# Two attention blocks on one core: reciprocals as exp(-ln) on ScalarE, the first rows of x in two halves, and new thresholds for the order of work

## The chip, the core and the metric

The kernel runs on one core of a Trainium2 chip. Its engines run side by side, each through its own list of instructions in order: TensorE (PE in the profile; PEld is its weight load), VectorE (DVE), ScalarE (ACT), GpSimd (POOL) and SyncE (SP), which here only issues DMAs. They wait for one another by semaphores. The metric is the device time of one execution in microseconds (us).

## The reference

Two independent blocks read their own x of 2048 rows by 512 columns; their results stand side by side in the output. Both have 32 heads of width 16.

```python
# A: softmax attention
scores = einsum("bhqd,bhkd->bhqk", q, k) * Dh ** -0.5
o = einsum("bhqk,bhkd->bhqd", softmax(scores), v);  a = o @ wo
# B: linear attention with learned features
phi_q = concat([softmax(q @ w_phi), softmax(-(q @ w_phi))]);  phi_k likewise
kv = einsum("bhsf,bhsd->bhfd", phi_k, v);  z = phi_k.sum over s
o = (phi_q @ kv) / (phi_q @ z + 1e-6);  b = o @ wo
```

Block A is nearly all of the work: 32 x 2048 x 2048 scores, each computed, put through an exponential, and summed.

## The kernel before, in words

**Block A.** Heads are taken four at a time (8 groups g). A *unit* is one group with a stretch of 128 or 256 queries; there are 73. Each unit goes through two passes over its scores, because the exponential needs the row maximum first.

- *Pass D*: PE computes scores with queries on the partitions (line 971), 512 keys to a PSUM bank, and DVE reduces one bank or two at a time to row maxima (line 1084, tile `part`). For some query blocks ("z") ACT first takes half of the work (`zS`, line 1011) and DVE joins it (line 1078).
- The maxima of a unit are joined on GpSimd, transposed by DMA and written as extra rows into the masked queries `QZ`, so that the next pass gets score minus maximum out of the matmul itself.
- *Pass E*: PE computes the scores again with keys on the partitions (line 1234), and ACT writes the exponential of one or two banks into a ring of 34 tiles `pT` (line 1246).
- *PV*: PE multiplies `pT` with the values, which carry a column of ones, so that the row sum comes out as a 17th row (line 1324).
- `finish_unit` then evacuates the result to `X`, moves the row sums by DMA into a compact tile `lr` (line 1381), takes their reciprocal on DVE (line 1384: 128 x 8 elements for a unit of 256 queries, 128 x 4 for one of 128), spreads them by five DMAs over `Yd`, and GpSimd multiplies `X` by `Yd` into `QT` (line 1403), where the output projection (line 1419) reads them. `X`, `lr` and `Yd` have two buffers each, one for even units and one for odd. The last three units go by `finish_last`, with a reciprocal of 128 x 128 straight from PSUM (line 1356).

**Block B** runs in the shadow of block A from about 240 us on, mostly on GpSimd. In `q_norm`, GpSimd adds 1e-6 to the 32 denominators of each row (`den_t`, line 1793), DVE takes the reciprocal (line 1795, 128 x 32), and GpSimd multiplies (line 1798). This happens 16 times.

**The start.** SP loads x in five pieces (two of 256 rows, three of 512) and the rest of the weights; ACT's queue loads the first columns of the weights for K and Q. PE runs six idle matmuls, turns the first 512 rows (line 374), DVE and ACT copy the four results (lines 381 and 383), and then the projections of K and Q for these rows (line 710), the masked queries of the first three units (`first_qz`, line 734), and the first scores follow. `pad_copy` (line 361) spreads the weights of Q and K into padded tiles.

**What sets the order.** From 7.6 us on the order on every engine is written by an *account* (`_Account`, made when the kernel is built). It keeps a clock for each engine, with a cost in us for each kind of work, and appends an instruction to an engine's list when the account's clock says that it is free. `task` gives ACT, DVE, GpSimd and SP work with a priority (lower goes first); an evacuation may go to ACT or to DVE (`choose`). `pick_pe` and `fill_cand` decide what PE does next: scores of pass D or E, PV, a projection job, or a filling matmul. They read a table of thresholds, `TH0`, overlaid with one row of `TH` for every 60 us. Those that the text speaks of are: `SINGLE` and `ESINGLE` (how little queued work DVE or ACT must have before PE fills one bank instead of two), `DCAP` and `ECAP` (how much queued work is the most), `COL` and `INCOL` (how much work both must have before PE turns to PV and projections), `PV_START`, `PV_LOW` and `PVN` (how full the ring of `pT` must be), and `BAL` (when DVE takes an evacuation). Semaphore waits are derived from the same dependencies, so the order is fixed, and the times at run time are those of the chip.

Of the kernel before, what the change touches and what calls it, by code (L numbers as in the profile page):

```python
# [213 lines left out]
def bass_concat_heads__softmax_full_mha__linear_kernel_hedgehog__prompt_kernel(  # L214
# [21 lines left out]
    with contextlib.ExitStack() as es:  # L236
# [81 lines left out]
        t_wa = {}  # L318
# [9 lines left out]
        def load_x(name, b0, b1):  # L328
            t_xs[name] = P.dma("sp", dsem("xs%d" % name), lambda e: e.dma_start(
                xs[:, b0:b1, :], A_x[0][128 * b0:128 * b1, :].rearrange("(b p) n -> p b n", p=128)))  # L330
# [5 lines left out]
        load_x(2, 4, 8)  # L336
# [27 lines left out]
        t_wqp = pad_copy(WQp, 0, t_wq0)  # L364
# [5 lines left out]

        pe_idle(6, [t_zmv, t_ones])
        for rb in range(4):
            for ct in range(4):
                t_turn = P.op("pe", lambda e, rb=rb, ct=ct: e.matmul(
                    PS[:, ct, 128 * rb:128 * rb + 128], xs[:, rb, ct * 128:ct * 128 + 128], ident[:, :],
                    start=True, stop=True), [t_xs[rb // 2], t_ident] if ct == 0 else [])
        pe_idle(2)
        t_x0 = []
        for ct in range(4):
            if ct % 2 == 0:  # L380
                t_x0.append(P.op("dve", lambda e, ct=ct: e.tensor_copy(xAT[:, ct, 0:512], PS[:, ct, :]), [t_turn]))
            else:
                t_x0.append(P.op("act", lambda e, ct=ct: e.activation(
                    xAT[:, ct, 0:512], PS[:, ct, :], ACT.Copy), [t_turn]))
# [17 lines left out]
        for r in range(4):  # L402
# [8 lines left out]
            {'SINGLE': 1.013, 'ESINGLE': 1.026, 'ZBIAS': 0.274, 'DBIAS': 0.27, 'ZREST': 0.238},  # L411
            {'SINGLE': 0.647, 'UA': 0.441, 'RF': 0.465, 'REPM': 0.115, 'PV_LOW': 6, 'DCAP': 2.442, 'ZBIAS': 0.207, 'BAL': 68.611},
            {'SINGLE': 1.013, 'UA': 0.408, 'REPM': 0.215, 'LHI': 0.119, 'DCAP': 1.302, 'ECAP': 1.815, 'ZBIAS': 0.315, 'DBIAS': 0.27, 'BAL': -28.613},
            {'SINGLE': 1.157, 'UA': 0.408, 'RF': 0.436, 'REPM': 0.215, 'LHI': 0.03, 'PV_START': 5, 'PV_LOW': 5, 'DCAP': 1.302, 'ECAP': 1.815, 'ZBIAS': 0.315, 'BAL': -28.613},
            {'SINGLE': 0.287, 'UA': 0.425, 'RF': 0.532, 'REPM': 0.196, 'LHARD': 0.35, 'LHI': 0.119, 'DCAP': 1.302, 'ECAP': 1.815, 'ZBIAS': 0.315, 'DBIAS': 0.27, 'BAL': -27.419},
            {'SINGLE': 1.157, 'UA': 0.408, 'RF': 0.436, 'REPM': 0.214, 'LHARD': 0.383, 'LHI': 0.03, 'PV_START': 5, 'PV_LOW': 5, 'PVN': 3, 'DCAP': 1.322, 'ECAP': 1.904, 'ZBIAS': 0.315, 'BAL': -27.335},
            {'COL': 0.708, 'SINGLE': 1.157, 'UA': 0.441, 'REPM': 0.196, 'LHI': 0.065, 'PVN': 3, 'DCAP': 2.495, 'ECAP': 1.461, 'ZBIAS': 0.315, 'DBIAS': 0.27, 'BAL': -27.419},
            {'ESINGLE': 1.165, 'RF': 0.62, 'REPM': 0.196, 'LHI': 0.065, 'ECAP': 1.185, 'ZBIAS': 0.049, 'DBIAS': 0.27, 'BAL': -27.419, 'ZREST': -0.23},
            {'ESINGLE': 1.2, 'RF': 0.62, 'REPM': 0.196, 'LHI': 0.122, 'ECAP': 1.185, 'ZBIAS': 0.049, 'DBIAS': 0.27, 'BAL': -27.419, 'ZREST': -0.23},
            {'COL': 0.63, 'INCOL': 0.753, 'ESINGLE': 1.097, 'RF': 0.436, 'REPM': 0.196, 'LHI': 0.079, 'JOBHOLD': 20.274, 'DCAP': 2.036, 'ECAP': 1.185, 'ZBIAS': 0.034, 'DBIAS': 0.314, 'BAL': -27.419, 'ZREST': -0.23},  # L420
            {'COL': 0.487, 'INCOL': 0.753, 'SINGLE': 0.633, 'ESINGLE': 1.097, 'RF': 0.596, 'REPM': 0.196, 'LHI': 0.079, 'JOBHOLD': 20.274, 'DCAP': 2.036, 'ECAP': 1.185, 'ZBIAS': 0.034, 'DBIAS': 0.334, 'BAL': -27.419, 'ZREST': -0.23},
            {'COL': 0.63, 'INCOL': 0.753, 'SINGLE': 0.663, 'ESINGLE': 1.097, 'UA': 0.458, 'RF': 0.676, 'REPM': 0.196, 'LHARD': 0.355, 'LHI': 0.246, 'JOBHOLD': 14.826, 'PV_START': 5, 'DCAP': 2.036, 'ECAP': 1.276, 'ZBIAS': 0.072, 'DBIAS': 0.278, 'BAL': -30.019, 'ZREST': -0.23},
            {'COL': 0.53, 'INCOL': 0.753, 'SINGLE': 0.674, 'ESINGLE': 1.097, 'UA': 0.442, 'RF': 0.67, 'REPM': 0.369, 'LHARD': 0.317, 'LHI': 0.259, 'JOBHOLD': 12.459, 'PV_START': 5, 'DCAP': 2.021, 'ECAP': 1.276, 'ZBIAS': 0.129, 'DBIAS': 0.278, 'BAL': -37.649, 'ZREST': -0.23},
            {'COL': 0.35, 'INCOL': 0.753, 'SINGLE': 0.749, 'ESINGLE': 1.097, 'UA': 0.433, 'RF': 0.67, 'REPM': 0.369, 'LHI': 0.259, 'JOBHOLD': 25, 'PV_START': 5, 'ECAP': 1.276, 'ZBIAS': 0.391, 'DBIAS': 0.278, 'BAL': -37.649, 'ZREST': -0.23},
            {'COL': 0.53, 'INCOL': 0.753, 'SINGLE': 0.749, 'ESINGLE': 1.097, 'UA': 0.442, 'RF': 0.67, 'REPM': 0.369, 'LHI': 0.259, 'JOBHOLD': 17.436, 'PV_START': 5, 'ECAP': 1.276, 'ZBIAS': 0.129, 'DBIAS': 0.278, 'BAL': -37.649, 'ZREST': -0.23},
            {'COL': 0.486, 'INCOL': 0.753, 'SINGLE': 0.638, 'ESINGLE': 1.097, 'UA': 0.442, 'RF': 0.67, 'REPM': 0.348, 'LHI': 0.259, 'JOBHOLD': 17.436, 'PV_START': 5, 'ECAP': 1.276, 'ZBIAS': 0.129, 'DBIAS': 0.278, 'BAL': -30.554, 'ZREST': -0.23},
            {'COL': 0.486, 'INCOL': 0.753, 'SINGLE': 0.638, 'ESINGLE': 1.097, 'UA': 0.442, 'RF': 0.67, 'REPM': 0.189, 'LHI': 0.259, 'JOBHOLD': 17.436, 'PV_START': 5, 'ECAP': 1.276, 'ZBIAS': 0.129, 'DBIAS': 0.278, 'BAL': -30.554, 'ZREST': -0.23},
            {'COL': 0.486, 'INCOL': 0.753, 'SINGLE': 0.735, 'ESINGLE': 1.057, 'UA': 0.442, 'RF': 0.648, 'REPM': 0.21, 'LHI': 0.234, 'JOBHOLD': 17.436, 'DCAP': 2.479, 'ECAP': 1.276, 'ZBIAS': 0.129, 'DBIAS': 0.278, 'BAL': -37.429, 'ZREST': -0.23},
            {'COL': 0.657, 'INCOL': 0.753, 'SINGLE': 0.735, 'ESINGLE': 1.057, 'UA': 0.442, 'RF': 0.648, 'REPM': 0.21, 'LHI': 0.234, 'JOBHOLD': 13.418, 'DCAP': 2.479, 'ECAP': 1.171, 'ZBIAS': 0.129, 'DBIAS': 0.278, 'BAL': -30.554, 'ZREST': -0.23},
            {'COL': 0.486, 'INCOL': 0.753, 'SINGLE': 0.933, 'ESINGLE': 1.057, 'UA': 0.442, 'RF': 0.61, 'REPM': 0.21, 'LHARD': 0.251, 'LHI': 0.285, 'JOBHOLD': 17.436, 'DCAP': 2.479, 'ECAP': 1.356, 'ZBIAS': 0.119, 'DBIAS': 0.111, 'BAL': -37.429, 'ZREST': -0.23},  # L430
# [4 lines left out]
        K.now = 7.6  # L435
# [3 lines left out]
        for e in K.free:  # L439
            K.free[e] = 7.6  # L440
# [32 lines left out]
        bank_tok = {ct: t_x0[ct] for ct in range(4)}  # L473
# [147 lines left out]
        area = []  # L621
# [68 lines left out]
        def proj(kind, a, c, at, prio):  # L690
            if kind == "v":
# [11 lines left out]
            else:  # L703
# [4 lines left out]

                def mm(e, b, ct):
                    return e.matmul(PS[:, b, :], wpad[:, ct, g, :], xAT[:, ct, c * 512:(c + 1) * 512],  # L710
                                    start=(ct == 0), stop=(ct == 3))
# [11 lines left out]
            job(at, [(2, 512, mm), (2, 512, lambda e, b, i: mm(e, b, i + 2))], fin, deps, prio)  # L723
# [3 lines left out]
        def first_qz(b, t):  # L727

            col = 0
            for u in range(3):  # L730
                w = units[u][2]

                def run(eng, u=u, w=w, col=col):
# [3 lines left out]
                    if u == 2:  # L737
# [4 lines left out]
                col += w  # L742
            QTt[(0, 0)] = qz_t[2]
# [73 lines left out]

        early = [("k", 0, 0), ("q", 0, 0)]
# [5 lines left out]
        at = 7.6  # L824
# [546 lines left out]
        def finish_unit(u, pt, bank):  # L1371
            if u >= NU - LASTU:
# [11 lines left out]
            pw_t[u] = K.task("dve", (0.115, 0.22), lambda eng: P.op("dve", lambda e: e.reciprocal(  # L1384
                lr[:, ub, 0:n], lr[:, ub, 0:n]), toks(d2)), d2, prio=-3.0, name="rec")
# [404 lines left out]
        def q_norm(st, cx):  # L1790
# [4 lines left out]
            t2 = K.task("dve", (0.265, 0.38), lambda eng: P.op("dve", lambda e: e.reciprocal(  # L1795
# [285 lines left out]
```

## Time and profile before

| | |
|---|---|
| time, median of 3 runs | 1199.13 us (1198.91 to 1201.43) |
| profiled execution: its time, its span | 1199.05 us, 1197.3 us |
| busy PE, DVE, ACT, POOL | 1117.4, 1170.3, 1149.8, 821.8 us |
| granted clock of TensorE | 0.999 |
| DVE: row maxima, line 1084 | 1118 instructions, 1130.0 us |
| ACT: exponentials, line 1246 | 1573 instructions, 1027.7 us |
| ACT: evacuations, line 560, from 60 to 1140 us | 214 instructions, 113.2 us |
| DVE: evacuations, line 563, in the whole span | 2 instructions, 1.1 us |

How to read it: the profile is one execution, with a record (start and duration) for each instruction. Busy time is the union of an engine's records. Records of neighbouring instructions overlap by some tenths of a microsecond, so the distance from one start to the next is what an instruction takes from a full engine. In a group of instructions the columns are line, engine, operation, tiles, shapes and count, then busy us and mean ns of one, then the engine's idle time just before them and what ended it. In a row of a stage the number in brackets behind a busy time is the count of instructions.

### The profile page before, as it was taken

What the parts mean: (1) busy time and instruction counts of PE and PEld (TensorE: products, weight loads), DVE (VectorE), ACT (ScalarE), POOL (GpSimd) and SP (SyncE); (2) the same over time, 40 slices, a digit from 0 to 9 for tenths busy, and PEclk for the clock granted to TensorE, in tenths of its full rate; (3) what the DMA queues carried; (4) which work ended last, traced back from release to release, by engine and by line L of the source; (5) the groups of instructions that cost most, each with busy time, mean ns of one, the idle gap of its engine ahead of it and who ended that gap; (6) DMA issues with size and microseconds to landing.
All of it is one profiled execution on the core that took longest, in us unless ns stands there. A gap on an engine that the chain in (4) does not pass through costs nothing.

```text
span 1197.3 us, 32106 instructions
## 1 busy us (share of the span) xinstructions
PE 1117.4 (93%) x13025; PEld 468.9 (39%) x13025; DVE 1170.3 (98%) x1290; ACT 1149.8 (96%) x1891; POOL 821.8 (69%) x1636
## 2 busy tenths in 40 slices
PE   8998999998999999999999998999999998899998
PEld 3433333343334333333433333333333333345555
DVE  8999999999999999999999999999999999999995
ACT  5898999999999999999999999999999999999997
POOL 8511211227888888888787887888888888888860
PEclk9999999999999999999999999999999999999999
DMA  5011221210002001001000101121112111111120
GB/s 142 9 25 43 42 48 32 43 38 8 8 14 35 8 6 26 13 10 22 12 7 17 25 7 22 22 49 31 29 34 33 35 34 27 20 29 37 33 30 18
DMA packets 104119, 33.61 MB, mean 28 GB/s; under 512 B 86692, under 2 KB 103972, under 8 KB 103972
## 3 DMA queue, kind: packets, MB, share of 16 engines
q1 hardware_dynamic: 102916, 31.31, 13.4%
q8 instruction: 102, 1.67, 0.6%
q14 instruction: 45, 0.37, 0.1%
q10 hardware_dynamic: 1056, 0.26, 0.1%
HBM read 5.26 MB, written 4.19 MB: 8 GB/s over the span
## 4 chain that ended last, share of the span: by engine, by line
ACT 38%; DVE 33%; PE 23%; SPq 2%; issue 1%; POOL 1%; DMA 1%
ACT pT L1246 32%; DVE part L1084 32%; PE PS L1234 7%; PE PS L971 6%; PE PS L1324 5%; PE PS L1419 2%; ACT eB L1639 1%; ACT xAT L560 1%; PE PS L777 1%; ACT zS L1011 1%; ACT X L560 1%; SPq L1392 1%; ACT WQp L560 1%; POOL uB L1588 1%; PE PS L1563 0%
## 5 line engine op out<-in xcount | busy, mean ns | idle before, releaser
L1084 DVE TENSOR_REDUCE part<-PS 128x2 f32<-128x1024 f32 (+1 forms) x1118 | 1130.0, 1079 | 7.6 <-PE PS L971 5.2
L1246 ACT ACTIVATE pT<-PS 128x512 bf16<-128x512 f32 (+1 forms) x1573 | 1027.7, 797 | 21.3 <-PE PS L1234 17.9
L1234 PE MATMUL PS<-QZ,KT 64*128 64x256 bf16 (+1 forms) x4906 | 560.4, 259 | 40.9 <-ACT pT L1246 22.0
L971 PE MATMUL PS<-KT,QZ 64*128 64x512 bf16 x2139 | 484.5, 383 | 26.3 <-DVE part L1084 9.7
L1234 PEld LDWEIGHTS PS<-QZ,KT 64*128 64x128 bf16 x4906 | 245.5, 94 | 323.1 <-ACT pT L1246 161.4
L971 PEld LDWEIGHTS PS<-KT,QZ 64*128 64x128 bf16 x2139 | 126.2, 93 | 198.2 <-DVE part L1084 72.2
L1324 PE MATMUL PS<-pT,VP 128*17 128x256 bf16 (+1 forms) x4672 | 186.7, 261 | 0.9
L1403 POOL TENSOR_TENSOR QT<-X,Yd 128x256 bf16<-128x256 f32 (+1 forms) x70 | 46.8, 668 | 95.4 <-DMA Yd<-Yd 95.1
L1324 PEld LDWEIGHTS PS<-pT,VP 128*17 128x17 bf16 x4672 | 74.9, 88 | 95.2 <-issue 79.0
L1588 POOL TENSOR_TENSOR uB<-uB 128x256 f32<-128x256 f32 (+2 forms) x160 | 83.4, 522 | 10.1
L1591 POOL TENSOR_SCALAR uB<-uB 128x256 f32<-128x256 f32 (+2 forms) x128 | 82.6, 646 | 11.2
L1116 POOL TENSOR_TENSOR dm<-part 128x16 f32<-128x16 f32 (+1 forms) x66 | 15.7, 238 | 91.1 <-DVE part L1084 90.8
L915 POOL TENSOR_TENSOR QZ<-QT,mask 128x512 bf16<-128x512 bf16 (+1 forms) x70 | 65.9, 941 | 15.7 <-PE PS L1234 12.8
L1645 POOL TENSOR_TENSOR xAT<-eB 128x512 f32<-128x512 bf16 x32 | 36.9, 1152 | 40.8 <-ACT eB L1639 40.6
L1677 POOL TENSOR_TENSOR wA<-eB,rB 128x1024 bf16<-128x1024 bf16 x32 | 61.7, 1928 | 2.0
L560 ACT ACTIVATE xAT<-PS 128x512 f32<-128x512 f32 (+3 forms) x83 | 50.1, 617 | 4.4 <-PE PS L1443 2.9
L1648 POOL TENSOR_TENSOR xAT<-xAT 128x256 f32<-128x256 f32 x64 | 36.0, 563 | 5.0
L1563 PE MATMUL PS<-WKp,xBT 128*128 128x512 bf16 x128 | 36.4, 383 | 1.1 <-ACT pT L1246 0.5
L1639 ACT ACTIVATE eB<-uB 128x1024 bf16<-128x1024 f32 x32 | 36.0, 1124 | 0.0
L1419 PE MATMUL PS<-WOp,QT 128*128 128x512 bf16 x120 | 35.8, 384 | 0.1
L1588 POOL TENSOR_TENSOR uB<-xAT,mB 128x512 f32<-128x512 f32 x32 | 33.8, 1057 | 1.8
L1662 POOL TENSOR_TENSOR WQp<-rB,WQp 128x64 f32<-128x64 f32 x96 | 30.6, 319 | 6.4
(113 smaller groups left out, 752.4 us busy)
## 6 DMA issues: line engine op xcount, KB each, us to landing
out_dram<-xAT SPq DMA_DIRECT2D x31, 128.0 KB, 1.8
Yd<-Yd SPq DMA_DIRECT2D x220, 16.0 KB, 2.1
QT<-eB SPq DMA_DIRECT2D x60, 32.0 KB, 2.0
QZ<-mcols SPq DMA_DIRECT2D x110, 1.0 KB
pT<-in_A_x_dram SPq DMA_DIRECT2D x3, 512.0 KB, 7.5
KT<-eB SPq DMA_DIRECT2D x48, 32.0 KB, 2.0
mcols<-stage SPq DMA_TRANSPOSE x69, 2.2
Yd<-Yd SPq DMA_DIRECT2D x60, 8.0 KB, 1.9
```

What stands on the lines that cost most here:

```text
L560: return P.op("act", lambda e: e.activation(dst, src, ACT.Copy), tk)
L915: "pool", lambda e: e.tensor_tensor(QZ[:, u % NQZ, :, 0:w], QT[:, g, q0:q0 + w].unsqueeze(1).broadcast_to([128, 2, w]), mask2[:, 0, :].uns ...
L971: return e.matmul(PS[:, b, :], QZ[p:p + 64, u % NQZ, r % 2, qt * 128:qt * 128 + 128], KT[p:p + 64, g, kc * 512:(kc + 1) * 512], start=star ...
L1084: tk = P.op("dve", lambda e: e.tensor_reduce(o, banks_ap(banks), AX.X, ALU.max), dep)
L1234: tok = P.op("pe", lambda e, r=rs[k], b=banks[k], kt=kt, x=x: e.matmul(PS[:, b, x * w:(x + 1) * w], KT[64 * (r // 2):64 * (r // 2) + 64, g ...
L1246: tk = P.op("act", lambda e: e.activation(pT[:, s0:s0 + n, :] if n > 1 else pT[:, s0, :], banks_ap(banks), ACT.Exp, scale=0.25), dep)
L1324: tok = P.op("pe", lambda e, r=r, kt=kt, x=x, s=es_[r][1]: e.matmul(PS[32 * r:32 * r + 17, bank, 0:w], VP[:, kt, 4 * g + r, :], pT[:, s, x ...
L1419: return e.matmul(PS[:, b, :], QT[:, i, st * 128:(st + 1) * 128], WOp[:, i, :], start=(i == 0), stop=(i == 7))
L1588: return P.op("pool", lambda e: e.tensor_tensor(o, a, b, op), dep)
L1591: return P.op("pool", lambda e: e.tensor_scalar(o, o, 0.0, None, ALU.max), dep)
L1639: cx["e"] = K.task("act", (0.95, 1.07), lambda eng: P.op("act", lambda e: e.activation(eB[:], uB[:], ACT.Exp), toks(d3)), d3, prio=-0.5, n ...
L1677: cx["phi"] = K.task("pool", (1.95, 1.95 + PLAT), lambda eng: P.op("pool", lambda e: e.tensor_tensor(phiB[k].rearrange("p (g f) -> p g f", ...
```

## The change

1. In `finish_unit` and `q_norm` the reciprocal on DVE becomes two activations on ACT: `Ln`, then `Exp` with scale -1. The second waits for the first.
2. The first 512 rows of x are handled in halves of 256 rows: PE turns a half, DVE and ACT copy it (eight copies instead of four), and while the second half is on its way the projection of Q for the first 256 rows runs, before K's. `first_qz` makes the masked queries of units 0 and 1 from it, and that of unit 2 from a second, narrower projection. The copy of Q's weights stands on DVE between the two halves' copies, two idle matmuls are gone, and the third load of x waits on SP until the first has landed.
3. The account starts at 6.8 us instead of 7.6, with other fixed times for the loads; it counts the matmuls ahead of its start; and all rows of `TH` are new (`TH0` is the same).

```diff
-        def load_x(name, b0, b1):
+        def load_x(name, b0, b1, dep=()):
...
-        load_x(2, 4, 8)
+        load_x(2, 4, 8, [t_xs[0]])
...
         pe_idle(6, [t_zmv, t_ones])
-        for rb in range(4):
+        t_x0 = {}
+        for hf in range(2):
+            for rb in range(2 * hf, 2 * hf + 2):
+                for ct in range(4):
+                    t_turn = P.op("pe", lambda e, rb=rb, ct=ct, hf=hf: e.matmul(
+                        PS[:, 4 * hf + ct, 128 * (rb % 2):128 * (rb % 2) + 128],
+                        xs[:, rb, ct * 128:ct * 128 + 128], ident[:, :],
+                        start=True, stop=True), [t_xs[hf], t_ident] if ct == 0 else [])
             for ct in range(4):
...
-        pe_idle(2)
-        t_x0 = []
...
+                dst_x = xAT[:, ct, 256 * hf:256 * hf + 256]
+                src_x = PS[:, 4 * hf + ct, 0:256]
+                if ct % 2 == 0:
+                    t_x0[hf, ct] = P.op("dve", lambda e, o=dst_x, i=src_x: e.tensor_copy(o, i), [t_turn])
+                else:
+                    t_x0[hf, ct] = P.op("act", lambda e, o=dst_x, i=src_x: e.activation(o, i, ACT.Copy), [t_turn])
+            if hf == 0:
+                t_wqp = pad_copy(WQp, 0, t_wq0)
         for ct in range(4):
...
+            t_q0 = P.op("pe", lambda e, ct=ct: e.matmul(
+                PS[:, 0, 0:256], WQp[:, ct, 0, :], xAT[:, ct, 0:256], start=(ct == 0), stop=(ct == 3)),
+                [t_wqp, t_x0[0, 2], t_x0[0, 3]] if ct == 0 else [])
...
-            {'SINGLE': 1.013, 'UA': 0.408, 'REPM': 0.215, 'LHI': 0.119, 'DCAP': 1.302, 'ECAP': 1.815, 'ZBIAS': 0.315, 'DBIAS': 0.27, 'BAL': -28.613},
...
+            {'COL': 1.131, 'SINGLE': 0.364, 'UA': 0.442, 'RF': 0.494, 'ZBIAS': 0.17, 'DBIAS': 0.21, 'BAL': -77.157, 'ZREST': -0.094},
...
-        K.now = 7.6
+        K.now = 6.8
...
-        T_w2 = K.fixed(t_wa["v"], 9.8)
+        T_w2 = K.fixed(t_wa["v"], 10.2)
...
-        area = []
+        area = [(2.5, 1.9, 1.9), (4.3, 0.6, 0.44), (5.5, 0.6, 0.44), (6.2, 0.45, 0.45)]
...
+                c0 = 256 if (kind, g, c) == ("q", 0, 0) else 0
...
-            pw_t[u] = K.task("dve", (0.115, 0.22), lambda eng: P.op("dve", lambda e: e.reciprocal(
-                lr[:, ub, 0:n], lr[:, ub, 0:n]), toks(d2)), d2, prio=-3.0, name="rec")
+            ln = K.task("act", (0.062, 0.17), lambda eng: P.op("act", lambda e: e.activation(
+                lr[:, ub, 0:n], lr[:, ub, 0:n], ACT.Ln), toks(d2)), d2, prio=-3.0, name="rec")
+            pw_t[u] = K.task("act", (0.062, 0.17), lambda eng: P.op("act", lambda e: e.activation(
+                lr[:, ub, 0:n], lr[:, ub, 0:n], ACT.Exp, scale=-1.0), toks([ln])), [ln], prio=-3.0, name="rec")
...
-            t2 = K.task("dve", (0.265, 0.38), lambda eng: P.op("dve", lambda e: e.reciprocal(
-                den_t[:, :], den_t[:, :]), [t1.tok]), [t1], prio=-1.0, name="rec")
+            ln = K.task("act", (0.08, 0.19), lambda eng: P.op("act", lambda e: e.activation(
+                den_t[:, :], den_t[:, :], ACT.Ln), [t1.tok]), [t1], prio=-1.0, name="rec")
+            t2 = K.task("act", (0.08, 0.19), lambda eng: P.op("act", lambda e: e.activation(
+                den_t[:, :], den_t[:, :], ACT.Exp, scale=-1.0), toks([ln])), [ln], prio=-1.0, name="rec")
```

`SINGLE` in the rows of `TH` for the stages from 120, 180, 240, 300 and 360 us is 1.013, 1.157, 0.287, 1.157 and 1.157 before, and 0.364, 0.42, 0.364, 0.364 and 0.364 after; in the three rows from 420 us on it is 0.619 before (by `TH0`) and 0.364 after.

More of the change, by code (lines that the diff above doesn't have):

```diff
@@ L428, in bass_concat_heads__softmax_full_mha__linear_kernel_hedgehog__prompt_kernel @@
[L428 to L430 removed]
+            {'ESINGLE': 0.802, 'ZBIAS': 0.286, 'DBIAS': 0.25},
@@ L431, in bass_concat_heads__softmax_full_mha__linear_kernel_hedgehog__prompt_kernel @@
+            {'COL': 0.749, 'INCOL': 0.872, 'SINGLE': 0.657, 'ESINGLE': 0.897, 'LHARD': 0.235, 'JOBHOLD': 22.798, 'DCAP': 2.718, 'ZBIAS': 0.317, 'DBIAS': 0.079},
+            {'UA': 0.403, 'REPM': -0.086, 'BAL': -37.9},
+            {'INCOL': 1.088, 'UA': 0.454},
         ]
@@ L472, in bass_concat_heads__softmax_full_mha__linear_kernel_hedgehog__prompt_kernel @@
         free_banks = list(range(NBANK))
-        bank_tok = {ct: t_x0[ct] for ct in range(4)}
+        bank_tok = {4 * hf + ct: t_x0[hf, ct] for hf in range(2) for ct in range(4)}
+        free_banks.remove(0)
         pe_mode = [None]
@@ L690, in proj @@
         def proj(kind, a, c, at, prio):
+            c0 = 0
             if kind == "v":
@@ L722, in fin, with first_qz @@
                                            engs=("act",), name="K")
-            job(at, [(2, 512, mm), (2, 512, lambda e, b, i: mm(e, b, i + 2))], fin, deps, prio)
+            job(at, [(2, 512 - c0, mm), (2, 512 - c0, lambda e, b, i: mm(e, b, i + 2))], fin, deps, prio)
         qz_t = {}
-        def first_qz(b, t):
-            col = 0
-            for u in range(3):
+        def first_qz(b, t, us):
+            for u in us:
                 w = units[u][2]
+                col = units[u][1]
                 def run(eng, u=u, w=w, col=col):
@@ L816, in turn @@
             job(at, [(4, 128, mm)], fin, [T_xs[c]], prio)
+        held.add(0)
+        first_qz(0, T_q0, [0, 1])
         early = [("k", 0, 0), ("q", 0, 0)]
```

65 lines of the change are left out of this document (28 added, 37 removed).

## The prediction

> **What bounds the kernel now.** I read the page's busy shares first, then the same shares by stage, then the waits, groups and timeline of the engine that proves full.
>
> ```profile
> PE 1117.4 (93%) x13025; PEld 468.9 (39%) x13025; DVE 1170.3 (98%) x1290; ACT 1149.8 (96%) x1891; POOL 821.8 (69%) x1636
> ACT 38%; DVE 33%; PE 23%; SPq 2%; issue 1%; POOL 1%; DMA 1%
> ```
> ```profile
> core 0: us, PE busy (x) PEld busy (x) DVE busy (x) ACT busy (x) POOL busy (x), PEclk, DMA share, GB/s
> 0.00:60.00 60.00, 56.13 (x475) 23.29 (x479) 53.76 (x65) 43.50 (x70) 40.07 (x49) 1.00 0.30 75
> 60.00:120.00 60.00, 52.81 (x649) 21.08 (x641) 57.95 (x62) 53.84 (x81) 10.53 (x26) 1.00 0.14 34
> ```
> ```profile
> 60.00:1140.00 1080.00, 1010.41 (x11428) 414.12 (x11420) 1072.36 (x1148) 1056.02 (x1740) 761.78 (x1546) 1.00 0.13 26
> 1140.00:1181.00 41.00, 39.71 (x777) 23.85 (x773) 40.18 (x72) 40.56 (x74) 19.44 (x40) 1.00 0.19 27
> 1181.00:1197.30 16.30, 11.19 (x364) 7.64 (x361) 4.02 (x8) 9.76 (x12) 0.46 (x1) 0.95 0.07 20
> ```
> Two engines look full. The stage 60 to 1140 us tells them apart: VectorE (DVE) is idle 1080 - 1072.4 = 7.6 us (0.7%), ScalarE (ACT) 24.0 us. The chain of waits changes between ACT 38%, DVE 33% and PE 23%, so no one engine carries it. ACT's spare time is larger than its idle time, because a record lasts longer than its place in the queue. The timeline of ACT (start, duration) shows that:
>
> ```profile
> 609.32 1.02 ACT L1246 ACTIVATE pT<-PS 128x1024 bf16<-128x1024 f32 x1
> 610.22 0.61 ACT L560 ACTIVATE xAT<-PS 128x512 f32<-128x512 f32 x1
> 610.70 1.04 ACT L1246 ACTIVATE pT<-PS 128x1024 bf16<-128x1024 f32 x1
> ```
> ```profile
> 1171.55 0.32 ACT L560 ACTIVATE X<-PS 128x128 f32<-128x128 f32 x1
> 1171.72 0.64 ACT L1246 ACTIVATE pT<-PS 128x512 bf16<-128x512 f32 x1
> 1172.20 0.45 ACT L560 ACTIVATE WQp<-PS 128x272 f32<-128x272 f32 x1
> 1172.47 1.58 ACT L1246 ACTIVATE pT<-PS 128x512 bf16<-128x512 f32 x2
> ```
> From one start to the next: 1024 columns 0.90 us, 512 columns 0.48, 272 columns 0.27, 128 columns 0.17. Each record is 0.12 to 0.18 longer than its place, so a gap that short never shows as idle. What ACT needs between 60 and 1140 us:
>
> ```profile
> L1246 ACT ACTIVATE pT<-PS 128x512 bf16<-128x512 f32 x1033 | 578.1, 672 | 4.1 <-PE PS L1234 2.1
> L1246 ACT ACTIVATE pT<-PS 128x1024 bf16<-128x1024 f32 x442 | 465.2, 1082 | 16.1 <-PE PS L1234 15.1
> L1639 ACT ACTIVATE eB<-uB 128x1024 bf16<-128x1024 f32 x31 | 34.9, 1126 | 0.0
> ```
> ```profile
> L1011 ACT ACTIVATE zS<-PS 128x1024 bf16<-128x1024 f32 x20 | 20.7, 1046 | 0.6 <-PE PS L978 0.2 <-PE PS L971 0.2
> ```
> ```profile
> 60.00:1140.00 1080.00, 113.21 (x214) 1.00 0.13 26
> ```
> (The last row is line 560, the evacuations.) 1033 x 0.48 + 442 x 0.90 = 893.6; evacuations 113.2 - 214 x 0.13 = 85.4; the rest 55.6 - 51 x 0.1 = 50.5. Sum 1029.5, so ACT has about 50 us to spare in this stage where DVE shows 7.6. DVE sets the pace; ACT waits for what DVE's maxima release.
>
> **The change, part by part.**
>
> *Reciprocals off DVE.* The row of line 1384 (count; shortest, median and longest in ns; first and last start; forms), two groups (busy, mean ns, idle before), and DVE's timeline:
>
> ```profile
> L1384 DVE RECIPROCAL lr<-lr x70: 145/190/200, 66.3 to 1176.0; 128x8 f32<-128x8 f32 x55, 128x4 f32<-128x4 f32 x15
> ```
> ```profile
> L1384 DVE RECIPROCAL lr<-lr 128x8 f32<-128x8 f32 x55 | 10.5, 191 | 0.0
> ```
> ```profile
> L1795 DVE RECIPROCAL den_t<-den_t 128x32 f32<-128x32 f32 x16 | 5.4, 338 | 0.0
> ```
> ```profile
> 611.27 1.21 DVE L1084 TENSOR_REDUCE part<-PS 128x2 f32<-128x1024 f32 x1
> 612.40 0.19 DVE L1384 RECIPROCAL lr<-lr 128x8 f32<-128x8 f32 x1
> 612.51 1.17 DVE L1084 TENSOR_REDUCE part<-PS 128x2 f32<-128x1024 f32 x1
> ```
> ```profile
> 1175.97 0.17 DVE L1384 RECIPROCAL lr<-lr 128x4 f32<-128x4 f32 x1
> 1176.06 0.32 DVE L1795 RECIPROCAL den_t<-den_t 128x32 f32<-128x32 f32 x1
> 1176.30 1.22 DVE L1084 TENSOR_REDUCE part<-PS 128x1 f32<-128x512 f32 x2
> ```
> Places in the queue: 0.11, 0.09 and 0.24 us. 55 x 0.11 + 15 x 0.09 + 16 x 0.24 = **11.2 us** leave DVE, all on the engine that sets the pace. The three reciprocals of the last units (line 1356) stay.
>
> *Ln and Exp on ACT.* 70 + 16 pairs, 172 instructions, an operation (Ln) that this trace does not show. By the line through 0.90 and 0.48 (0.00082 us a column, 0.06 fixed) 8 columns take 0.07 and 32 take 0.09: 140 x 0.07 + 32 x 0.09 = **12.7 us**. Lower end: 172 x 0.06 = 10.3. Upper end: each holds ACT for the 0.32 us of the shortest record above, 55 us, as if Exp, which waits for Ln's semaphore, always found nothing to run in between. I take 12.7, since in the account any ready exponential may slip between the two and ACT always has a queue. It lies in ACT's 50 us, so it costs the path nothing; without that cover it would cost its 12.7 us whole. Behind each waiting Ln or Exp stand ACT's exponentials; the new waits are for a DMA (row sums) or GpSimd (denominators), and the old reciprocals, with the same waits, show 0.0 idle before them in the two groups above.
>
> The Trainium skill ("ScalarE: Activation LUTs", section "What ACT_TABLE_LOAD costs") gives 186 ns + 0.833 ns a column, neighbours overlapping by 93 ns. That is a fixed 0.09 where the trace's line has 0.06; by it the pairs would be an estimated 17.8 us, still inside the 50.
>
> The chain behind (two DMAs, the multiply of line 1403) gets an Exp and perhaps one exponential later, under 1.2 us. GpSimd's multiply feeds only the output projection and buffers two units old, one unit taking (1176.0 - 66.3) / 69 = 16 us; I cost it at nothing. SP gets no new DMA in the loop.
>
> *The start.* Timeline of PE, DVE and ACT:
>
> ```profile
> 5.47 0.62 PE L374 MATMUL PS<-ident,pT 128*128 128x128 bf16 x8 [0.59 <-DMA pT<-in_A_x_dram]
> 5.93 0.59 PE L368 MATMUL PS<-zmv,ones_t 128*128 128x512 bf16 x2
> 7.48 1.04 PE L710 MATMUL PS<-xAT,WKp 128*128 128x512 bf16 x4 [0.95 <-DVE xAT L381]
> 8.35 1.03 PE L710 MATMUL PS<-xAT,WQp 128*128 128x512 bf16 x4
> ```
> ```profile
> 5.84 0.29 DVE L361 COPY WQp<-wA 128x512 bf16<-128x512 bf16 x1 [0.93 <-DMA wA<-in_A_wqkv_dram]
> 6.13 1.29 DVE L381 CAST xAT<-PS 128x512 bf16<-128x512 f32 x2
> 9.42 1.35 DVE L734 TENSOR_TENSOR QZ<-PS,mask 128x256 bf16<-128x256 f32 x3 [2.00 <-PE PS L710]
> 10.69 1.21 DVE L1084 TENSOR_REDUCE part<-PS 128x2 f32<-128x1024 f32 x1
> ```
> ```profile
> 8.55 0.69 ACT L559 ACTIVATE KT<-PS,bias_k 128x512 bf16<-128x512 f32 x1 [1.34 <-PE PS L710]
> ```
> Today Q follows K on PE, and the first masked queries wait until 9.42. Afterwards the first 256 rows are copied while the second 256 arrive; their Q runs at about 6.2 (weights 5.84 + 0.29), K at about 6.8 when the second copies end. K is 0.7 earlier, the masked queries are ready before K's evacuation (about 8.5), and the first reduction moves from 10.69 to about 9.3. Against that the third load of x, and on SP all loads behind it, wait for the first to land (about 4.2). Gain between 0 (the next loads come late and eat it) and 1.4; I take **1.0**, as the loads share bandwidth anyway. Eight half copies for four whole ones, the second part of Q and the two dropped idle matmuls lie on engines that are waiting here, so nothing.
>
> *Thresholds.* They order the work, and add none. SINGLE decides when DVE may take one bank instead of two; for 120 to 240 and 300 to 420 us it falls from 1.0-1.2 to about 0.4. The first row below is of 300 to 420 us, the second of 420 to 660:
>
> ```profile
> L1084 DVE TENSOR_REDUCE part<-PS 128x1 f32<-128x512 f32 x64 | 40.4, 676 | 0.0
> ```
> ```profile
> L1084 DVE TENSOR_REDUCE part<-PS 128x1 f32<-128x512 f32 x12 | 7.8, 682 | 0.0
> ```
> A pair takes 1.13 (611.27 to 612.40), two singles 2 x (0.676 - 0.08) = 1.19. Some 58 singles too many in 120 us are 29 x 0.06 = 1.7 us, and the stage before is alike: 0 to 3 us, I take **2**.
>
> *Given back.* Once DVE is relieved, ACT's spare falls to 50 - 12.7 = 37, less the 13 by which the stage shrinks: 24 of 1067 us, 2.2%. DVE's own gap is 0.7% now; two engines equally full can't both find PE ready, so it ends between 0.7% (nothing given back) and 2.2% (16 us). I take **5 us**, nearer the row that DVE has now.
>
> Sum: -11.2 - 1.0 - 2.0 + 5.0 = -9.2 us against the profiled execution, 1199.05 (span 1197.3 and 1.75 around it; the median, 1199.13, is the same within 0.1): **1189.9 us**. The tail after the last maximum (1181 to 1197.3) is as before.
>
> **Rivals.**
> 1. *All of it stays.* DVE's gap keeps its 0.7%: 1199.05 - 14.2 = 1184.9. For it: DVE kept that through 18 stages. Against: ACT has less room.
> 2. *Nothing is left.* DVE's gap goes to 2.2%: -14.2 + 16 = +1.8, 1197 to 1201. For it: ACT is in 38% of the chain; moved work is not removed work.
> 3. *Slower: Exp sits waiting for Ln on ACT.* At 0.32 us an instruction ACT gains 55 us, has 50 to spare, and becomes the pace; with DVE's 7.6 as its own gap: 1199.05 - 1.0 + 55 - 50 + 7.6 = 1210.6. It decides from about 0.25 us an instruction (172 x 0.25 = 43). For it: the explicit wait; against: ACT's full queue. A poor order by the new thresholds ends on the same side: DVE idle all through as it is from 60 to 120 us (60 - 57.95 = 2.05 per 60, so 37 us over the 18 such stages of the middle instead of 7.6) is 29 - 14 = +15, about 1214.
> 4. *A table load at every Ln and Exp.* The trace has one load, 1.28 us at the start, for a set named for logarithm and exponential; 172 more are 220 us, some 1376.
>
> The Trainium skill ("ScalarE: Activation LUTs", section "Table sets: the hidden batching unit") says that Ln then Exp need one load when that set is used, which speaks against the fourth; this trace, without any Ln, can't show it.
>
> **How the numbers follow.** Forecast case (1186 to 1196) 0.48; the first rival 0.17; the second 0.13; the third with the poor order 0.20; the fourth 0.02. 0.2% is 2.4 us, about what a measurement here tells from no change. Faster 0.48 + 0.17 = 0.65, same 0.13, slower 0.22. The range 1182 to 1204 takes in the first two rivals and a little of the third (0.48 + 0.15 + 0.13 + 0.05 = 0.81); the likeliest case alone is 1186 to 1196.
>
> **What would show it.** Right: no reciprocal on DVE before the last units, first reduction near 9.3 us, fewer single reductions at 120 to 420 us, DVE's idle at most 1.2% in the middle, ACT's rows of 128x8 starting 0.07 apart from their successors, one table load. Wrong: ACT idle directly before Exp, waits of ACT for DMA or GpSimd, DVE waiting for PE at line 971 far above 5 us, or scores kept back at the start by late loads of x.

## The result, and the profile after

The changed kernel takes 1208.56 us (median of 4 runs, 1207.49 to 1211.0) against 1199.8 us for the kernel before in the same comparison: ratio 1.0068, 95% interval [1.0055, 1.0081]. It is slower by 0.7%, some 8 us, where 9 us less were forecast. Its profiled execution has a span of 1207.1 us. Two rows of its page, the busy shares and the chain of waits by engine:

```profile
PE 1118.8 (93%) x13022; PEld 460.3 (38%) x13022; DVE 1169.0 (97%) x1165; ACT 1161.1 (96%) x2092; POOL 822.0 (68%) x1636
ACT 49%; PE 27%; DVE 22%; issue 1%; POOL 0%; DMA 0%; POOLq 0%
```

VectorE has 125 instructions fewer and is busy almost as long as before; ScalarE has 201 more and is busy 11 us longer; the chain has moved from VectorE (33% to 22%) to ScalarE (38% to 49%).

That VectorE is busy almost as long has a reason in the thresholds. Its 86 reciprocals are gone, but the new order gives it 22 evacuations (11.1 us of records) where the kernel before has 2 (1.1 us). The two largest groups of them:

```profile
L573 DVE CAST xAT<-PS 128x512 bf16<-128x512 f32 x6 | 4.1, 685 | 1.0 <-PE PS L1832 0.9
L573 DVE COPY WQp<-PS 128x272 f32<-128x272 f32 x7 | 2.9, 433 | 0.2 <-PE PS L1796 0.2
```

With the new start but the old thresholds it has 4 after the first reduction, with the new ones 20. ScalarE has lost these 20 evacuations and got, besides Ln and Exp, 47 more exponentials, because 47 pairs of banks were split in two. By stage:

```profile
60.00:1020.00 960.00, 895.11 (x9465) 347.56 (x9460) 952.67 (x907) 939.33 (x1714) 651.88 (x1308) 1.00 0.12 25
1020.00:1080.00 60.00, 53.67 (x790) 23.54 (x787) 52.34 (x56) 59.88 (x92) 49.74 (x107) 1.00 0.16 29
```

The columns are those of the stages of the kernel before. In the stage from 1020 to 1080 us VectorE idles for 7.7 us while ScalarE is full. The same stage of the kernel before:

```profile
1020.00:1080.00 60.00, 54.16 (x796) 25.07 (x796) 59.15 (x66) 59.50 (x92) 50.42 (x112) 1.00 0.14 25
```

There VectorE idles for 0.9 us. VectorE's timeline around one half of that idle time, and GpSimd's waits for a masked-query buffer after and before:

```profile
1036.31 6.94 DVE L1099 TENSOR_REDUCE part<-PS 128x2 f32<-128x1024 f32 x7
1047.20 0.69 DVE L1099 TENSOR_REDUCE part<-PS 128x1 f32<-128x512 f32 x1 [3.95 <-PE PS L986]
```
```profile
POOL QZ L930 <- PE PS L1249: 46.0, 16, 13.7
```
```profile
POOL QZ L915 <- PE PS L1234: 12.8, 6, 8.7
```

Line 930 makes the masked queries `QZ` of a unit, and there are four buffers; it waits for pass E of the unit four back. GpSimd's idle time there (total us, times, longest) has risen from 12.8 to 46.0 us. So VectorE's maxima run further ahead of ScalarE's exponentials here, up to the fourth buffer. This comes with the new written order and not with the relief of VectorE. Two runs that are told below show it: the first row is the changed order with the reciprocals back on VectorE, the second the kernel before without its reciprocals.

```profile
POOL QZ L930 <- PE PS L1249: 45.5, 16, 13.7
POOL QZ L915 <- PE PS L1234: 12.5, 6, 8.7
```

The hole near 1047 us belongs to the order too: with the reciprocals back on VectorE it still idles for 7.0 us in that stage. The longer lead shows at the end, where ScalarE works off what VectorE has left it. From the last row maximum to the end the kernel before takes 16.4 us (nearly the stage from 1181 us in the prediction), the changed kernel 21.5:

```profile
1185.50:1207.10 21.60, 15.11 (x533) 10.58 (x521) 5.34 (x11) 14.39 (x18) 0.45 (x1) 1.00 0.08 23
```

The other rows that the prediction named: the first reduction (start, duration of three), the new instructions in a full stretch of ScalarE with their largest groups, and the groups of row maxima.

```profile
9.31 3.49 DVE L1099 TENSOR_REDUCE part<-PS 128x2 f32<-128x1024 f32 x3
```

```profile
601.37 0.23 ACT L1399 ACTIVATE lr<-lr 128x8 f32<-128x8 f32 x1
601.47 0.62 ACT L1261 ACTIVATE pT<-PS 128x512 bf16<-128x512 f32 x1
601.94 0.24 ACT L1401 ACTIVATE lr<-lr 128x8 f32<-128x8 f32 x1
602.04 1.05 ACT L1261 ACTIVATE pT<-PS 128x1024 bf16<-128x1024 f32 x1
```
```profile
L1401 ACT ACTIVATE lr<-lr 128x8 f32<-128x8 f32 x55 | 14.6, 265 | 0.2
L1399 ACT ACTIVATE lr<-lr 128x8 f32<-128x8 f32 x55 | 14.5, 263 | 0.5 <-DMA lr<-X 0.5
```
```profile
L1099 DVE TENSOR_REDUCE part<-PS 128x2 f32<-128x1024 f32 x903 | 1036.4, 1219 | 8.8 <-PE PS L986 6.1 <-PE PS L1249 0.4 <-PE PS L993 0.3
L1099 DVE TENSOR_REDUCE part<-PS 128x1 f32<-128x512 f32 x154 | 100.8, 685 | 5.0 <-PE PS L986 4.4
```

Ln (line 1399) and Exp (line 1401) take 0.10 us each, with an exponential run in between. Added up from start to next start over all 172 they are 19.5 us (15.5 for the row sums, 4.0 for the denominators). Single reductions fell from 276 to 154.

### The profile page after: what moved, and what is told of

It reads as the page before. It is cut to its first block, busy times and chain, and to the rows that moved or that the text cites. A ratio compares the mean times of both kernels' runs of the same rounds, so it can differ in the third digit from the quotient of the medians.

```text
span 1207.1 us, 32204 instructions
## 1 busy us (share of the span) xinstructions
PE 1118.8 (93%) x13022; PEld 460.3 (38%) x13022; DVE 1169.0 (97%) x1165; ACT 1161.1 (96%) x2092; POOL 822.0 (68%) x1636
## 3 DMA queue, kind: packets, MB, share of 16 engines
q1 hardware_dynamic: 102916, 31.31, 12.7%
## 4 chain that ended last, share of the span: by engine, by line
ACT 49%; PE 27%; DVE 22%; issue 1%; POOL 0%; DMA 0%; POOLq 0%
ACT pT L1261 41%; DVE part L1099 21%; PE PS L1249 8%; PE PS L986 7%; PE PS L1339 6%; ACT xAT L570 2%; PE PS L1436 2%; ACT eB L1656 1%; PE PS L707 1%; ACT zS L1026 1%; PE PS L1580 1%; ACT X L570 1%; PE PS L723 1%; ACT vB L570 0%; PE PS L1730 0%
## 5 line engine op out<-in xcount | busy, mean ns | idle before, releaser
L1249 PE MATMUL PS<-QZ,KT 64*128 64x256 bf16 (+1 forms) x4774 | 548.6, 259 | 41.5 <-ACT pT L1261 23.1
L986 PE MATMUL PS<-KT,QZ 64*128 64x512 bf16 x2078 | 457.9, 383 | 28.5 <-DVE part L1099 13.9
L1249 PEld LDWEIGHTS PS<-QZ,KT 64*128 64x128 bf16 x4774 | 240.2, 94 | 315.8 <-ACT pT L1261 161.3
L986 PEld LDWEIGHTS PS<-KT,QZ 64*128 64x128 bf16 x2078 | 119.7, 93 | 201.3 <-DVE part L1099 81.9
L1608 POOL TENSOR_SCALAR uB<-uB 128x256 f32<-128x256 f32 (+2 forms) x128 | 82.6, 645 | 11.2
L570 ACT ACTIVATE xAT<-PS 128x512 f32<-128x512 f32 (+2 forms) x76 | 45.3, 619 | 4.2 <-PE PS L1460 3.2
L1605 POOL TENSOR_TENSOR uB<-mB,xAT 128x512 f32<-128x512 f32 x32 | 33.8, 1057 | 2.1
```

The source lines that it names most:

```text
L570: return P.op("act", lambda e: e.activation(dst, src, ACT.Copy), tk)
L986: return e.matmul(PS[:, b, :], QZ[p:p + 64, u % NQZ, r % 2, qt * 128:qt * 128 + 128], KT[p:p + 64, g, kc * 512:(kc + 1) * 512], start=star ...
L1249: tok = P.op("pe", lambda e, r=rs[k], b=banks[k], kt=kt, x=x: e.matmul(PS[:, b, x * w:(x + 1) * w], KT[64 * (r // 2):64 * (r // 2) + 64, g ...
L1605: return P.op("pool", lambda e: e.tensor_tensor(o, a, b, op), dep)
L1608: return P.op("pool", lambda e: e.tensor_scalar(o, o, 0.0, None, ALU.max), dep)
```

## The experiments

Two theories stood at first. *A*: ScalarE sets the pace in both kernels, and the short gaps before its exponentials are no spare time. *B*: VectorE does set it, as predicted, and the new order of work lost what the move had won. After the first four runs a third was formed, *A2*: PE's written order feeds both engines, so they advance together, at each place at the pace of the fuller one; both are full in the kernel before. Ratios are to the kernel before, run beside each.

**Four runs with the order of every engine kept.** The account plans as it did; only what is issued at a place differs.

Reciprocals left out of the kernel before (the same for `t2` with `t1.tok`):

```diff
-            pw_t[u] = K.task("dve", (0.115, 0.22), lambda eng: P.op("dve", lambda e: e.reciprocal(
-                lr[:, ub, 0:n], lr[:, ub, 0:n]), toks(d2)), d2, prio=-3.0, name="rec")
+            pw_t[u] = K.task("dve", (0.115, 0.22), lambda eng: lr_t[u].tok, d2, prio=-3.0, name="rec")
```

> The kernel before, every engine's order of instructions unchanged, but the 86 reciprocals on VectorE (lines 1384 and 1795) left out, so rows and denominators are multiplied by the sum instead of divided. This takes 11.2 us off VectorE and nothing off ScalarE. Theory of the prediction (VectorE sets the pace of the kernel before): 11 us faster, about 1188. Theory A (ScalarE sets it, and its short gaps before an exponential are no spare time): at most 3 us faster, 1197 to 1200. Theory B (VectorE does set it, and the changed kernel lost its time to its new order of work): as the prediction, about 1188.

Measured: ratio 1.0004 [0.9994, 1.0014]. Taking 11.2 us off VectorE and putting nothing anywhere is worth nothing. The chain of this run, to be held against that of the kernel before in the prediction:

```profile
ACT 51%; PE 29%; DVE 16%; SPq 2%; issue 1%; DMA 1%; POOL 0%; POOLq 0%
```

VectorE's share falls from 33% to 16% and ScalarE's rises from 38% to 51%. What VectorE no longer does it waits out: its idle time from 60 to 1140 us is 13.0 us here (7.6 before).

```profile
60.00:1140.00 1080.00, 1009.37 (x11388) 413.45 (x11386) 1067.03 (x1066) 1054.71 (x1737) 762.44 (x1543) 1.00 0.13 26
```

Small exponentials added on ScalarE in the kernel before, beside each reciprocal:

```diff
+        def two_small(n):
+            for k in range(2):
+                i = len(small_t)
+                small_t.append(P.op("act", lambda e, i=i: e.activation(
+                    scr[:, i % 6, 0:n], ones_t[:, 0:n], ACT.Exp), [t_ones, small_t[i - 6] if i >= 6 else None]))
```

> The kernel before, order unchanged, reciprocals kept on VectorE, and beside each of the 86 two small exponentials on ScalarE that read a constant tile, write a scratch tile and wait for nothing (8, 4 or 32 columns): 172 x about 0.10 us = 17 us more on ScalarE, nothing more on VectorE. Theory of the prediction and theory B (ScalarE has 50 us to spare): within 3 us, 1197 to 1203. Theory A: 12 to 17 us slower, 1212 to 1217.

Measured: 1.0095 [1.0078, 1.0113], 11.4 us. The 172 instructions take 18.2 us from start to next start, so 63% of what is put on ScalarE shows. Their largest group (with no idle time before it) and the chain:

```profile
L1420 ACT ACTIVATE scr<-ones_t 128x8 bf16<-128x8 bf16 x110 | 20.3, 275 | 0.0
```
```profile
ACT 58%; PE 24%; DVE 12%; POOL 3%; issue 2%; SPq 1%; DMA 1%
```

Of the 50 us to spare, 18.2 us of work found room for only 6.8.

Ln left out of the changed kernel:

```diff
-            ln = K.task("act", (0.062, 0.17), lambda eng: P.op("act", lambda e: e.activation(
-                lr[:, ub, 0:n], lr[:, ub, 0:n], ACT.Ln), toks(d2)), d2, prio=-3.0, name="rec")
+            ln = K.task("act", (0.062, 0.17), lambda eng: lr_t[u].tok, d2, prio=-3.0, name="rec")
```

> The changed kernel, order unchanged, but the 86 Ln left out, so Exp gives exp of minus the sum itself: about 9.7 us less on ScalarE by the records (7.7 + 1.9). Theory A: 8 to 10 us faster than the changed kernel, 1198 to 1201. Theory B (the new order lost the time): 1206 to 1209, as the changed kernel.

Measured: 1.0013 [1.0004, 1.0022], against 1.0068 with Ln: 6.6 us for 9.7 us of ScalarE. Theory B, for which nothing should have changed, falls; theory A expected a little more, 8 to 10 us.

Reciprocals back on VectorE in the changed kernel's order (Ln issues nothing, Exp's place issues this):

```diff
+            pw_t[u] = K.task("act", (0.062, 0.17), lambda eng: P.op("dve", lambda e: e.reciprocal(
+                lr[:, ub, 0:n], lr[:, ub, 0:n]), toks([ln])), [ln], prio=-3.0, name="rec")
```

> The changed kernel, order unchanged, but at the place of each pair of Ln and Exp one reciprocal on VectorE, as in the kernel before: 19.5 us less on ScalarE, 11.2 us more on VectorE. Theory A: 14 to 19 us faster than the changed kernel, 1190 to 1195, which is below the kernel before too. Theory B: no faster than the changed kernel, 1207 to 1219.

Measured: 1.0055 [1.0040, 1.0070], some 1.6 us below the changed kernel, which the intervals don't tell apart. ScalarE is 19.5 us lighter, and it helps little, because now VectorE carries the chain:

```profile
DVE 73%; PE 16%; ACT 7%; SPq 1%; issue 1%; POOL 1%; DMA 1%; ACTq 0%; POOLq 0%
```

This was a miss for theory A, which has ScalarE as the only bound, and the reason for A2.

**Three more with the order kept, for A2.** Ln, Exp and reciprocals all left out of the changed kernel (as the run without Ln, and then the same for Exp):

```diff
-            pw_t[u] = K.task("act", (0.062, 0.17), lambda eng: P.op("act", lambda e: e.activation(
-                lr[:, ub, 0:n], lr[:, ub, 0:n], ACT.Exp, scale=-1.0), toks([ln])), [ln], prio=-3.0, name="rec")
+            pw_t[u] = K.task("act", (0.062, 0.17), lambda eng: ln.tok, [ln], prio=-3.0, name="rec")
```

> The changed kernel, order unchanged, with Ln and Exp both left out and no reciprocal in their place, so rows and denominators are multiplied by the sum. 19.5 us less on ScalarE, nothing more on VectorE. Theory A2 (PE's written order ties the two engines: at each place the fuller one sets the pace; the changed kernel is slow because ScalarE got 19.5 us, and its order leaves VectorE idle for 8 us near 1050 us): another 3 to 6 us below the run without Ln, ratio to the kernel before 0.996 to 0.999, when VectorE has become the limit in turn. Theory A (ScalarE alone): 1.0013 - 0.008, ratio 0.993. Theory B (the new order lost all): as without Ln, 1.001 or above.

Measured: 0.9989 [0.9979, 0.9998], within A2's span. It closes the sum for the changed kernel. From here, putting Ln and Exp on ScalarE costs 1.0068 - 0.9989 = 0.8%, 9.5 us (half of their 19.5); putting the reciprocals on VectorE instead costs 1.0055 - 0.9989 = 0.7%, 7.9 us (of 11.2). And against the kernel before without its reciprocals (1.0004) it is 0.15% better, 1.8 us: that is all that the new start, the thresholds and the pairing brought together, with the evacuations moved to VectorE and the longer end in it, and the two intervals overlap a little.

Next, ScalarE alone and then both engines relieved in the kernel before; the second run has this edit and that of the run without reciprocals:

```diff
             def run(eng):
+                if name == "yB" and len(deps) > 1:
+                    return deps[0].tok
                 tk = toks(deps) + ([t_bias] if bias is not None else [])
```

> The kernel before, order unchanged, reciprocals kept, but 30 of the 32 evacuations of block B's numerators (128 x 272, name yB, from about 760 us on) left out on ScalarE, so block B's output is of the first rows only: 30 x 0.277 = 8.3 us less on ScalarE, nothing less on VectorE. Theory A (ScalarE alone sets the pace): 6 to 8 us faster, ratio 0.993 to 0.995. Theory A2 (PE's order ties the two, and both are full): VectorE becomes the limit, 0 to 3 us, ratio 0.997 to 1.000.

> The same with the reciprocals on VectorE left out as well, so that both engines are relieved (8.3 us of ScalarE from about 760 us on; 11.2 us of VectorE, some 8 of them in that stretch). Theory A2: what neither does alone comes now, 4 to 8 us faster, ratio 0.993 to 0.997. Theory A: the same as the run with the evacuations alone left out.

Measured: 0.9984 [0.9973, 0.9995] for ScalarE alone (8.3 us off, 1.9 us gained) and 0.9961 [0.9947, 0.9976] for both (4.7 us gained). VectorE alone had given nothing. Relief of both gives more than the two reliefs apart (0.0 and 1.9), as A2 says, but the surplus of 0.0027 is little more than the intervals of the three runs together (some 0.002), and it is only some half of the load taken. The chains, ScalarE alone relieved and then both:

```profile
DVE 51%; ACT 26%; PE 19%; issue 1%; SPq 1%; DMA 1%
```
```profile
ACT 45%; PE 26%; DVE 25%; issue 2%; SPq 1%; DMA 1%; POOL 0%
```

**Where VectorE's time went.** The traces of these runs answer that. Count each instruction of VectorE from its first to its last row maximum at the distance from start to start that is usual for its form in the kernel before, or in the changed one where that has none (1.131 us for a pair of banks, 0.598 for a single one). What is left of the stretch is waiting. Times in us, one profiled execution each; executions of one kernel spread over up to 5 us, so differences of 1 or 2 mean nothing here.

| | first reduction at | VectorE's instructions | its waits | from the last maximum to the end |
|---|---|---|---|---|
| kernel before | 10.7 | 1156.9 | 12.6 | 16.4 |
| the same, no reciprocals | 10.9 | 1145.5 | 25.1 | 16.7 |
| changed kernel | 9.3 | 1148.3 | 27.2 | 21.5 |
| the same, reciprocals on VectorE | 9.3 | 1159.7 | 16.2 | 21.7 |
| the same, no reciprocals, no Ln and Exp | 9.2 | 1148.3 | 19.8 | 21.7 |

The 11.4 us that the reciprocals leave free in the kernel before come back as 12.5 us of waits. In the changed kernel VectorE's instructions take 8.6 us less and its first reduction comes 1.4 us earlier, but its waits grow by 14.6 us and the end by 5.1: together 9.7 us more, the difference of the two spans. The longer end is there with and without Ln and Exp.

**Five runs with the order written anew.** They were meant to try the parts of the change one at a time, and taught something else. The first, second and fourth missed what A2 expected of them. Ln and Exp alone, in the kernel before (and the same for `t2`):

```diff
-            pw_t[u] = K.task("dve", (0.115, 0.22), lambda eng: P.op("dve", lambda e: e.reciprocal(
-                lr[:, ub, 0:n], lr[:, ub, 0:n]), toks(d2)), d2, prio=-3.0, name="rec")
+            ln = K.task("act", (0.062, 0.17), lambda eng: P.op("act", lambda e: e.activation(
+                lr[:, ub, 0:n], lr[:, ub, 0:n], ACT.Ln), toks(d2)), d2, prio=-3.0, name="rec")
+            pw_t[u] = K.task("act", (0.062, 0.17), lambda eng: P.op("act", lambda e: e.activation(
+                lr[:, ub, 0:n], lr[:, ub, 0:n], ACT.Exp, scale=-1.0), toks([ln])), [ln], prio=-3.0, name="rec")
```

> The kernel before with nothing but the reciprocals as Ln and Exp on ScalarE; the order is written anew by the account with the old thresholds and the old start. Theory A2: 8 to 14 us slower than before, ratio 1.007 to 1.012, as with the 172 small exponentials (1.0095), whatever VectorE saves. Theory B (thresholds or start are to blame): 0.998 to 1.002.

Measured: 1.0234 [1.0219, 1.0249]. The start in halves alone, that is the changed kernel with two edits taken back, these lines (and those of `t2`) and all rows of `TH`:

```diff
-            ln = K.task("act", (0.062, 0.17), lambda eng: P.op("act", lambda e: e.activation(
-                lr[:, ub, 0:n], lr[:, ub, 0:n], ACT.Ln), toks(d2)), d2, prio=-3.0, name="rec")
-            pw_t[u] = K.task("act", (0.062, 0.17), lambda eng: P.op("act", lambda e: e.activation(
-                lr[:, ub, 0:n], lr[:, ub, 0:n], ACT.Exp, scale=-1.0), toks([ln])), [ln], prio=-3.0, name="rec")
+            pw_t[u] = K.task("dve", (0.115, 0.22), lambda eng: P.op("dve", lambda e: e.reciprocal(
+                lr[:, ub, 0:n], lr[:, ub, 0:n]), toks(d2)), d2, prio=-3.0, name="rec")
...
-            {'ESINGLE': 0.802, 'ZBIAS': 0.286, 'DBIAS': 0.25},
+            {'SINGLE': 1.013, 'ESINGLE': 1.026, 'ZBIAS': 0.274, 'DBIAS': 0.27, 'ZREST': 0.238},
...
```

> The kernel before with nothing but the start in two halves (account from 6.8 us), reciprocals on VectorE, old thresholds, order written anew. Theory A2: the first reduction comes 1.4 us earlier and that is gained, ratio 0.998 to 1.000. Theory B with the start to blame: above 1.003.

Measured: 1.0199 [1.0183, 1.0214]. Ln and Exp with the start, under the old thresholds, so only the second of these two edits:

> The changed kernel (Ln and Exp on ScalarE, start in two halves) with the old thresholds, order written anew. If the new thresholds are what brings the changed kernel near the old one: 1.015 to 1.035, well above its 1.0068. If the new thresholds do harm: below 1.005.

Measured: 1.0224 [1.0207, 1.0241]. Start and new thresholds, with the reciprocals on VectorE, so only the first:

> The changed kernel with its start and its thresholds, but the reciprocals on VectorE as tasks of the account, so that the order is written anew. Theory A2: 4 to 10 us faster than the changed kernel, ratio 0.998 to 1.003, about level with the kernel before. Theory B: 1.005 to 1.010.

Measured: 1.2033 [1.2015, 1.2051]. Here block B came late, and GpSimd worked it off nearly alone at the end (columns as in the stages):

```profile
1180.00:1444.30 264.30, 87.49 (x1230) 41.24 (x1238) 64.53 (x112) 60.31 (x87) 210.89 (x373) 0.60 0.14 29
```

Three changes as different as these all lose some 2% under the old thresholds, so they can't be read as the price of Ln and Exp or of the start. The last run checks that directly:

```diff
-            pw_t[u] = K.task("dve", (0.115, 0.22), lambda eng: P.op("dve", lambda e: e.reciprocal(
+            pw_t[u] = K.task("dve", (0.111, 0.21), lambda eng: P.op("dve", lambda e: e.reciprocal(
```

> The kernel before with one number of the account changed and nothing else: the cost of the row-sum reciprocal is 0.111 and 0.21 us instead of 0.115 and 0.22. The work is the same, only the written order can differ. Theory A2 with thresholds fitted to one order: 5 to 30 us slower, ratio 1.004 to 1.025, as in the other orders written anew. If the order is robust: 0.999 to 1.001, and then the 27 us of Ln and Exp under the old thresholds belong to ScalarE's work itself.

Measured: 1.0142 [1.0127, 1.0157]. The same computation, with 4 ns less of busy time and 10 ns less of latency in the account's cost of one kind of task, is 17 us slower. Its middle stage, and its chain:

```profile
60.00:1140.00 1080.00, 991.65 (x11068) 414.29 (x11141) 1057.95 (x1161) 1040.15 (x1671) 750.66 (x1519) 1.00 0.13 25
```
```profile
ACT 48%; PE 28%; DVE 13%; POOL 6%; issue 3%; DMA 1%; SPq 0%; ACTq 0%
```

VectorE idles 22.0 us there instead of 7.6, ScalarE 39.9 instead of 24.0. The thresholds fit one written order, not the kernel in general. The changed kernel needed its own, and they brought it from 1.0224 to 1.0068.

What stays open: how much of the 0.15% is the earlier start and how much the new thresholds, since no run could move one without writing the order anew; and whether a longer search for thresholds would have made up the rest. No version tried with the whole computation in it beats the kernel before.

## Why the prediction was wrong

- **"DVE sets the pace; ACT waits for what DVE's maxima release."** This step failed. VectorE's 0.7% of idle time was read as the bound and ScalarE's 2.2% as slack. The kernel before without reciprocals (1.0004) shows that VectorE's work was not what set the end: it ends no earlier and waits longer for PE. Nor was it the maxima that held back the exponentials: in the kernel before, PE's pass E waited 1.3 us in all for maxima written to `QZ`, and 22.0 us for ScalarE itself (the rows give total us, times and longest). In the chain of waits, ScalarE's 38% stood ahead of VectorE's 33%; the prediction saw this and passed over it.

```profile
PE PS L1234 <- ACT pT L1246: 22.0, 66, 0.5
PE PS L1234 <- DMA QZ<-mcols: 1.3, 1, 1.3
```

- **"ACT has about 50 us to spare."** This is the number that carried the wrong sign. 50 us is what remains when each instruction takes its shortest distance to the next. (The 7.6 us that they are held against are idle time; by distances VectorE waits for 12.6.) But work put into the queue hardly fills that remainder: 18.2 us of independent small instructions cost 11.4 us. The trace shows what it consists of: from 60 to 1140 us 269 instructions of ScalarE start over 0.03 us later than is usual behind the one before, 57 us in all, and for every one the semaphore of PE that it waits for came within 0.03 us of its start. Ahead of 218 of them (47 us) PE's records have no gap for 1.5 us. So PE itself, busy for 94% of this stage, looks like a third nearly full engine. That would also explain why relief of both others gives only some half, but the ends of PE's records are modelled and no run took work off PE alone: it is not shown.
- **11.2 us off VectorE.** The move was as described (no reciprocal before the last units); the gain was 0, because the time became waiting for PE (12.6 to 25.1 us in the kernel before without reciprocals).
- **12.7 us on ScalarE.** Mis-sized: 19.5 us measured, 0.098 us for 8 columns and 0.119 for 32 instead of 0.07 and 0.09. The line was drawn through instructions that read PSUM and extended to ones that read SBUF. The Trainium skill ("ScalarE: Activation LUTs", "What ACT_TABLE_LOAD costs"), by whose figures the estimate was 17.8 us, was nearer; its 186 - 93 + 0.833 x 8 = 100 ns agrees with the 98 here. The larger number alone would not have changed the forecast, since the 50 us would still have covered it.
- **"Thresholds. They order the work, and add none."** This failed too. They moved 20 evacuations to VectorE, 8.3 us by the count above, which takes back most of the 11.2. Single reductions fell as forecast (276 to 154); this saved 3.9 us, where 2 were taken.
- **The start.** Right as a sequence: the first reduction at 9.31 us (9.3 forecast, 10.69 before). As a gain of 1.0 us it is at most part of the 0.15%.
- **Given back, 5 us.** The mechanism was named (two engines equally full, served by one PE), but it was set small. VectorE's idle time from 60 to 1140 us rose by 8.0 us, from 7.6 to 15.6 (1.4%), and its waits from the first to the last maximum by 14.6 us. Of these some 7 us go with Ln and Exp, since they fall to 19.8 without them.
- **The tail after the last maximum, as before.** Wrong, and it was a term put at nothing: 21.5 us against 16.4. The four kernels in the changed order have 21.5 to 21.7 us, with and without Ln and Exp, and the five in the order of the kernel before 16.4 to 16.7. So the longer end comes from the order.
- **The rivals.** The first is excluded. The second came closest to the mechanism, but it stopped at level. The third gave the right sign for a wrong reason: Exp does not sit waiting for Ln (line 1401 shows 0.2 us of idle time in all, and another instruction stands between the two in 81 of 86 pairs), and the price was far under the 0.25 us an instruction named as the turning point; with so little room to spare there was no turning point. Its other form, a poor new order, is seen in the hole and the longer end, but not in the sum: with all reciprocals out, the new order is no worse than the old (0.9989 and 1.0004). The fourth is excluded: the trace has one table load of 1.28 us, as before. There it agrees with the Trainium skill ("ScalarE: Activation LUTs", "Table sets: the hidden batching unit").

## What to carry to other kernels

Here two engines were busy for 98% and 96% of the span, with one in-order PE feeding both, and idle time was not slack: relief of the fuller one alone gave nothing, load on the other showed by 63%, and relief of both gave most. Test "is there room on this engine?" by adding small independent instructions to it with the order kept, before moving work there, and "does this engine's time matter?" by leaving work out. When the order is new, count first which engine got which work: here the thresholds gave VectorE back most of what was taken off it. Where an order comes from a planner with fitted thresholds, a change of a cost can write a new order: here a few nanoseconds cost 1.4%, so parts of a change can be compared only with the order held fixed.

## What the runs showed of the hardware that was not expected

ScalarE's fixed cost per instruction differs here with where it reads. From start to next start in full stretches, 1024 columns read from PSUM take 0.90 us, as the prediction shows, while 1024 columns read from SBUF take 0.95; here is one from the kernel before:

```profile
606.66 1.07 ACT L1639 ACTIVATE eB<-uB 128x1024 bf16<-128x1024 f32 x1
607.61 0.40 ACT L560 ACTIVATE X<-PS 128x256 f32<-128x256 f32 x1
```

Together with 0.098 us at 8 columns and 0.119 at 32 (both SBUF), and with 0.48 us at 512 and 0.27 at 272 (both PSUM), this is 0.83 ns a column plus some 0.09 us from SBUF and 0.05 us from PSUM. The reciprocals of VectorE in the kernel before took 0.084, 0.109 and 0.259 us from start to start for 4, 8 and 32 columns, which is 6.25 ns a column plus 0.06 us. So for 8 columns the reciprocal was cheaper than Ln and Exp (2 x 0.10), and for 32 columns about as dear (2 x 0.12).
